# Transposing keys and queries by DMA in a fused retention and FFN kernel, with a rewoven start

## The chip, the cores and the metric

The kernel runs on one core of a Trainium2 chip. Profiles call the engines PE (TensorE, the matrix unit), DVE (VectorE), ACT (ScalarE), POOL (GpSimd) and SP (which here only issues DMAs). The metric is device time in microseconds (us), the median of several executions. The kernel before takes 228.82 us (three runs, 228.13 to 229.55). A run counts as slow, and is left out of comparisons, when it lies over 1.5% above the fastest run of the same kernel.

## The reference, cut to what matters

Four sequences of 768 tokens and 8 heads of 64 go through a retention recurrence, and its output goes through an FFN with a squared ReLU.

```python
for t in range(S):                       # per head, gamma = 1 - 2**(-5-h)
    state = gamma * state + outer(k[t], v[t])
    y[t] = scale * q[t] @ state
h = np.maximum(x @ w_in, 0.0)            # x: 3072 x 512, w_in: 512 x 2048
return h * h @ w_out                     # w_out: 2048 x 512
```

## The kernel before

The 3072 tokens are 24 chunks of 128. For a chunk, k is scaled and cast on VectorE (K), q is cast, and k and q are turned so that the head dimension lies on the partitions (T: eight PE transposes and one eviction by ScalarE). Scores are taken and masked (S), and output and state follow (P). The FFN works on blocks of 2, 2, 1, 3, 4, 4, 4 and 4 chunks: F is one row group of `x @ w_in`, G one quarter of `h*h @ w_out` for one chunk. Strings of these letters give the order of the program, and the engines are read here as running in it (the timeline below shows `K1`'s cast on VectorE at 10.73 us, `S0`'s multiply at 11.33); Z is a filler matmul on zeros, Y fills decay factors, L loads.

```python
    def a_turn(m):
        ...
        for x, src in enumerate((a["ks"], a["qs"])):
            for p in range(NP):
                nc.tensor.transpose(tp[:, x, p, :], src[:, 2 * p : 2 * p + 2, :], ident[:])
        nc.scalar.activation(kqT[:], tp[:], AF.Copy)
    ...
    run("Y0 Z12 K0 T0 Y1 Z2 K1 S0 Z2 T1 P0 K2 S1 Y2 Z2 T2")
    load_w_in(0)
    load_w_in(1)
    run("P1 K3 S2 Y3 Z2 T3 P2 S3 Y4 Z4")
    for s in (2, 3):
        load_w_in(s)
    for s in range(NSL):
        w = load_w_out(s)
    ...
    weave(
        all_f1(3) + all_f2(3),
        [... "K8 T8 K9,S8 L10,T9 K10,P8 S9 L11,T10 K11,P9 S10 L12,T11 L13,P10 S11 L14,P11 K12,T12 L15,S12,K13" ...],
    )
```

Note `K1 S0`: the k cast of the next chunk stands ahead of the scores whose mask multiply also runs on VectorE.

## Time and profile before

| | kernel before |
|---|---|
| time, median | 228.82 us |
| span of the profiled run | 225.9 us |
| PE busy | 212.3 us |
| first FFN matmul | 19.46 us |
| fifth block's FFN (512 columns) starts | 94.64 us |
| TensorE clock granted | 1.000 |

The prediction below shows the busy row, the chain and the waits. One more view matters later, the page's 40 slices of the span. PEclk is the clock granted to TensorE in each, in tenths of full speed, 9 being 90% or more.

```profile
PEclk9999999999999999999999999999999999999999
```

The clock is full throughout. How VectorE orders the start shows in the timeline (start, length, engine, line, operation; brackets hold the idle time before it):

```profile
10.73 0.68 DVE L192 SCALAR_TENSOR_TENSOR ks_272<-kn_116,kf 128x512 bf16<-128x512 f32 x1
10.78 0.40 PE L227 MATMUL st_278<-kqT_239 64*128 64x128 bf16 x8 [0.65 <-ACT kqT_239 L218]
...
11.33 1.22 DVE L235 TENSOR_TENSOR pt_287<-st_278,cmask 128x1024 bf16<-128x1024 f32 x1
```

The cast of the next chunk's k (10.73) comes before the mask multiply of these scores (11.33). The next chunk is turned while the multiply runs (its transposes start at 11.55 and 12.10 us, the multiply ends at 12.55); scores come every 3.2 to 3.5 us (7.59, 10.78, 14.32, 17.86).

### The profile page before, as it was taken

The numbers are of one execution on the slowest core, as the hardware profiler recorded it, in microseconds if no ns is written. First come the engines' busy times: TensorE is split into PE (matmuls) and PEld (weight loads), VectorE is DVE, ScalarE is ACT, GpSimd is POOL, SyncE is SP. The second block draws the span as 40 slices with busy tenths as digits, with TensorE's granted clock in tenths as the row PEclk, the third lists the DMA queues.
The fourth block names the chain that finished last, engine by engine and source line by source line (L and its number), as shares of the span: only waits on it lengthen the run. The fifth ranks groups of instructions, "written<-read, shape, count | busy, mean of one in ns | idle before, by whom it ended". The sixth has DMA issues, their size and how long they took to land.

```text
span 225.9 us, 4271 instructions
## 1 busy us (share of the span) xinstructions
PE 212.3 (94%) x1736; PEld 117.5 (52%) x1736; DVE 103.2 (46%) x221; ACT 123.1 (54%) x246; POOL 43.5 (19%) x62
## 2 busy tenths in 40 slices
PE   7677899998879999999999999999999999999993
PEld 2444785456646664445455555455454555444441
DVE  4574664127835964175650275740275704144000
ACT  6798883156637862377623477524467532367121
POOL 3275000439752433030330310000000000000000
PEclk9999999999999999999999999999999999999999
DMA  7999999989999999477729973013200011200112
GB/s 168 256 209 204 205 200 202 248 219 189 166 177 205 171 80 147 73 183 45 49 57 130 118 167 22 3 46 93 94 2 0 3 46 46 96 0 0 46 46 93
DMA packets 82579, 25.43 MB, mean 113 GB/s; under 512 B 75392, under 2 KB 79488, under 8 KB 82560
## 3 DMA queue, kind: packets, MB, share of 16 engines
q0 software_dynamic: 37504, 8.39, 40.7%
q1 hardware_dynamic: 45056, 16.78, 28.6%
q8 instruction: 13, 0.21, 0.4%
q14 instruction: 6, 0.05, 0.1%
HBM read 27.26 MB, written 6.29 MB: 149 GB/s over the span
## 4 chain that ended last, share of the span: by engine, by line
PE 84%; DMA 5%; ACT 4%; SPq 3%; DVE 2%; issue 1%; POOL 0%; ACTq 0%
DMA w_in_bf_96<-in_moe_w_in_dram 3%; SPq L91 3%; DMA vn_120<-in_v_dram 2%; PE op_2633 L335 2%; PE op_1480 L335 2%; PE op_2223 L335 2%; PE op_2512 L335 2%; PE op_2317 L335 2%; PE op_1920 L335 2%; PE op_1826 L335 2%; PE op_1427 L335 2%; PE op_1072 L335 2%; PE op_2860 L335 2%; PE op_705 L335 2%; PE op_695 L335 2%; PE op_2820 L335 2%
## 5 line engine op out<-in xcount | busy, mean ns | idle before, releaser
L316 PEld LDWEIGHTS <-w_in_bf_96 128*128 128x128 bf16 x128 | 11.4, 98 | 10.3 <-issue 1.4
L316 PEld LDWEIGHTS <-w_in_bf_98 128*128 128x128 bf16 x128 | 11.8, 98 | 8.7
L316 PEld LDWEIGHTS <-w_in_bf_99 128*128 128x128 bf16 x128 | 11.6, 98 | 8.2
L316 PEld LDWEIGHTS <-w_in_bf_97 128*128 128x128 bf16 x128 | 11.4, 98 | 8.1
L324 DVE TENSOR_TENSOR h_0_442<-h_0_442 128x256 bf16<-128x256 bf16 x32 | 9.3, 293 | 7.1 <-ACT h_0_442 L323 3.2
L324 DVE TENSOR_TENSOR h_5_2687<-h_5_2687 128x512 bf16<-128x512 bf16 x16 | 6.8, 426 | 11.8 <-ACT h_5_2687 L323 11.8
L324 DVE TENSOR_TENSOR h_2_1544<-h_2_1544 128x512 bf16<-128x512 bf16 x16 | 6.8, 424 | 10.7 <-ACT h_2_1544 L323 10.6
L324 DVE TENSOR_TENSOR h_4_2348<-h_4_2348 128x512 bf16<-128x512 bf16 x16 | 6.8, 425 | 9.6 <-ACT h_4_2348 L323 9.6
L324 DVE TENSOR_TENSOR h_3_1951<-h_3_1951 128x512 bf16<-128x512 bf16 x16 | 6.8, 423 | 9.5 <-ACT h_3_1951 L323 9.5
L324 DVE TENSOR_TENSOR h_1_876<-h_1_876 128x128 bf16<-128x128 bf16 (+1 forms) x32 | 8.2, 287 | 4.5 <-ACT h_1_876 L323 4.4
L335 PEld LDWEIGHTS <-h_5_2687 128*128 128x128 bf16 x64 | 6.3, 98 | 7.6
L335 PEld LDWEIGHTS <-h_3_1951 128*128 128x128 bf16 x64 | 6.0, 98 | 7.1
L335 PEld LDWEIGHTS <-h_2_1544 128*128 128x128 bf16 x64 | 6.0, 98 | 7.1
L335 PEld LDWEIGHTS <-h_4_2348 128*128 128x128 bf16 x64 | 5.9, 97 | 6.9
L335 PEld LDWEIGHTS <-h_1_876 128*128 128x128 bf16 x64 | 6.0, 98 | 6.8
L335 PEld LDWEIGHTS <-h_0_442 128*128 128x128 bf16 x64 | 6.0, 98 | 6.6
L351 PE MATMUL fill<-zero 128*128 128x512 bf16 x24 | 8.3, 484 | 1.2 <-DVE zero L146 1.2
L344 ACT ACTIVATE osb_744<-op_695 128x512 f32<-128x512 f32 x1 | 0.6, 597 | 8.2 <-PE op_695 L335 8.2
L253 PEld LDWEIGHTS <-s_bd_175 128*128 128x128 bf16 x48 | 3.6, 98 | 2.3
L351 PEld LDWEIGHTS <-zero 128*128 128x128 bf16 x24 | 2.4, 119 | 4.6 <-issue 2.7
L206 POOL CAST qs_736<-qn_420 128x512 bf16<-128x512 f32 x1 | 0.6, 613 | 19.6 <-DMA qn_420<-in_q_dram 19.6
L235 DVE TENSOR_TENSOR pt_792<-st_783,cmask 128x1024 bf16<-128x1024 f32 x1 | 1.2, 1225 | 5.8 <-PE st_783 L227 5.8
(811 smaller groups left out, 522.2 us busy)
## 6 DMA issues: line engine op xcount, KB each, us to landing
w_in_bf_96<-in_moe_w_in_dram POOLq DMA_DIRECT2D x1, 512.0 KB, 7.0
w_in_bf_97<-in_moe_w_in_dram POOLq DMA_DIRECT2D x1, 512.0 KB, 8.6
w_in_bf_98<-in_moe_w_in_dram POOLq DMA_DIRECT2D x1, 512.0 KB, 9.0
w_in_bf_99<-in_moe_w_in_dram POOLq DMA_DIRECT2D x1, 512.0 KB, 10.8
w_out_bf_100<-in_moe_w_out_dram POOLq DMA_DIRECT2D x1, 512.0 KB, 12.9
w_out_bf_101<-in_moe_w_out_dram POOLq DMA_DIRECT2D x1, 512.0 KB, 14.7
w_out_bf_102<-in_moe_w_out_dram POOLq DMA_DIRECT2D x1, 512.0 KB, 16.6
w_out_bf_103<-in_moe_w_out_dram POOLq DMA_DIRECT2D x1, 512.0 KB, 18.5
```

Source lines behind the costliest of these rows:

```text
L91: return eng.dma_start(t[:], src[b, :, i * C : (i + 1) * C, :].rearrange("h s d -> s h d"))
L206: nc.gpsimd.tensor_copy(qs[m][:], qn.pop(m)[:])
L235: nc.vector.tensor_tensor(out=pt[:], in0=st[:], in1=cmask[:, None, None, :].to_broadcast([P, 2, NP, P]), op=ALU.mult,)
L253: nc.tensor.matmul(yt[:, p, :], lhsT=s_bd[i % 2][:, p, :], rhs=kqT[:, 1, p, :], start=(p == 0), stop=False, skip_group_check=True,)
L316: nc.tensor.matmul(hp[:, :n], lhsT=w_in_bf[s][:, cb, r * P : (r + 1) * P], rhs=xts[g][:, cb, cols], start=(cb == 0), stop=(cb == NCB - 1),)
L324: nc.vector.tensor_mul(h2[:, fb, cols], h2[:, fb, cols], h2[:, fb, cols])
L335: nc.tensor.matmul(op[:], lhsT=h2s[g][:, fb, j * P : (j + 1) * P], rhs=w_out_bf[part][:, r, :], start=(fb == 0), stop=(fb == NFB - 1),)
L344: nc.scalar.activation(osb[:], op[:], AF.Copy)
L351: nc.tensor.matmul(t[:], lhsT=zero[:, :P], rhs=zero[:], start=True, stop=True)
```

## The change

Its intent is to take the transposes of chunks 8 to 23 off PE, the bound. A DMA issued by SP turns k and q straight into place, from two slots ahead. In the start the transposes are split in halves (t for k, u for q), the decay factors become products on GpSimd, casts get their own letters (k, q, v), and the blocks of 2, 2, 1 and 3 chunks are woven anew. The diff, cut to its core:

```diff
-    def a_turn(m):                      # whole transposes for every chunk
+    def a_turn(m, x):                   # half: x = 0 k, x = 1 q; tp shares ps_f's four buffers
+    def dma_turn(m):
+        at[m] = kTpool.tile([P, 2, NP, P], BF16, tag="kqT", name=f"kqT{m}")
+        nc.sync.dma_start_transpose(
+            at[m][:].rearrange("d x p s -> d (x p) s"),
+            kq[m][:].rearrange("s x h d -> s (x h d)"),
+        )
     def fill_yf(i):
-        for p in range(NP):
-            nc.scalar.activation(yf[i][:, p, :], t_f[:, i * C : (i + 1) * C], AF.Exp, ...)
+        nc.gpsimd.tensor_tensor(out=yf[i][:], in0=yf[0][:], in1=gc[:, i, :, None]..., op=ALU.mult)
...
-    run("Y0 Z12 K0 T0 Y1 Z2 K1 S0 Z2 T1 P0 K2 S1 Y2 Z2 T2")
-    load_w_in(0)
+    run("Z10 Y1 k0 t0 q0 Z1 u0 v0 Z2 S0 Y2")
+    run("k1 Z2 t1 q1 Z1 u1 P0 v1 S1 Y3")
+    issue_behind(load_w_in(0), q2)
+    run("k2 Z2 t2 q2 Z1 u2 P1 v2 S2")
     load_w_in(1)
+    run("k3 Z2 t3 q3 Z1 u3 P2 v3 S3 Y4")
...
+    behind = load_w_out(1)
+    load_w_out(2)
...
+    issue_behind(load(nc.sync, "k", 4), behind)
+    q4 = load(nc.sync, "q", 4)
+    issue_behind(load_w_out(3), q4)     # fourth quarter of w_out behind q of chunk 4
...
+    run("k6 ... S6 k7 G4.1 t7 q7 v7 P6 G3.3 u7 G4.2 S7 L8 L9 G4.3 P7")
+    run("k8 X8 L10")
+        runs("k9 L11,X9,S8,k10 L12,X10,P8 S9,k11 L13,X11,P9 S10,k12 L14,X12,P10 S11,k13 X13 L15,P11 S12,k14 X14"),
```

X is the transposing DMA. Buffers move too: `ps_f` gets four (from three), the separate transpose buffer in PSUM goes, and the FFN's `hpool` gets two (from three). The q casts of chunks 4 to 7 move from GpSimd to VectorE. No run tests these two by themselves.

More of the change, by code (lines that the diff above doesn't have):

```diff
@@ L59 @@
     ldpool = ctx.enter_context(tc.tile_pool(name="ldpool", bufs=4))
-    bfpool = ctx.enter_context(tc.tile_pool(name="bfpool", bufs=7))
-    kpool = ctx.enter_context(tc.tile_pool(name="kpool", bufs=4))
+    bfpool = ctx.enter_context(tc.tile_pool(name="bfpool", bufs=8))
+    kTpool = ctx.enter_context(tc.tile_pool(name="kTpool", bufs=5))
     atpool = ctx.enter_context(tc.tile_pool(name="atpool", bufs=3))
     xtpool = ctx.enter_context(tc.tile_pool(name="xtpool", bufs=3))
-    hpool = ctx.enter_context(tc.tile_pool(name="hpool", bufs=3))
+    hpool = ctx.enter_context(tc.tile_pool(name="hpool", bufs=2))
     opool = ctx.enter_context(tc.tile_pool(name="opool", bufs=4))
     PS = bass.MemoryType.PSUM
-    ps_tp = ctx.enter_context(tc.tile_pool(name="ps_tp", bufs=1, space=PS))
     ps_st = ctx.enter_context(tc.tile_pool(name="ps_st", bufs=1, space=PS))
@@ L70 @@
     ps_c = ctx.enter_context(tc.tile_pool(name="ps_c", bufs=1, space=PS))
-    ps_f = ctx.enter_context(tc.tile_pool(name="ps_f", bufs=3, space=PS))
+    ps_f = ctx.enter_context(tc.tile_pool(name="ps_f", bufs=4, space=PS))
     w_in_v = moe_w_in.rearrange("(cb p) f -> p cb f", p=P)
@@ L77 @@
     w_out_bf = [const.tile([P, FPS, DM], BF16, name=f"w_out_bf{s}") for s in range(NSL)]
-    kn, qn, vn, qs, vs = {}, {}, {}, {}, {}
+    kn, qn, vn, kq, vs = {}, {}, {}, {}, {}
     FIRST = 8
@@ L84, in load @@
         src = {"k": k, "q": q, "v": v}[name]
+        if m not in kq:
+            kq[m] = bfpool.tile([P, 2, H, D], BF16, tag="kq", name=f"kq{m}")
+            vs[m] = bfpool.tile([P, H, D], BF16, tag="v", name=f"vs{m}")
         if name == "k" or m < FIRST:
@@ L87, in load @@
             {"k": kn, "q": qn, "v": vn}[name][m] = t
-        else:
-            t = bfpool.tile([P, H, D], BF16, tag=name, name=f"{name}s{m}")
-            {"q": qs, "v": vs}[name][m] = t
+            t = t[:]
+        elif name == "q":
+            t = kq[m][:, 1]
+        else:
+            t = vs[m][:]
         return eng.dma_start(
-            t[:], src[b, :, i * C : (i + 1) * C, :].rearrange("h s d -> s h d")
+            t, src[b, :, i * C : (i + 1) * C, :].rearrange("h s d -> s h d")
         )
@@ L114 @@
         load(nc.sync, "k", m)
-        load(nc.sync, "q", m)
+        ins = load(nc.sync, "q", m)
+        if m == 2:
+            q2 = ins
         load(nc.sync, "v", m)
@@ L120 @@
     nc.gpsimd.iota(ex_i[:], pattern=[[C, NCH], [0, H]], base=0, channel_multiplier=1)
-    t_i = const.tile([P, S], I32)
-    nc.gpsimd.iota(t_i[:], pattern=[[1, S]], base=0, channel_multiplier=0)
+    t_i = const.tile([P, C], I32)
+    nc.gpsimd.iota(t_i[:], pattern=[[1, C]], base=0, channel_multiplier=0)
+    eg_i = const.tile([P, NCH, NP], I32)
+    nc.gpsimd.iota(eg_i[:], pattern=[[C, NCH], [0, NP]], base=0, channel_multiplier=0)
     ident = const.tile([P, P], BF16)
@@ L164 @@
         nc.vector.memset(lnp[r, h // 2 : h // 2 + 1], float(np.log(gammas[h])))
-    t_f = const.tile([P, S], FP32)
+    t_f = const.tile([P, C], FP32)
     nc.vector.tensor_copy(t_f[:], t_i[:])
+    eg_f = const.tile([P, NCH, NP], FP32)
+    nc.vector.tensor_tensor(
+        out=eg_f[:],
+        in0=eg_i[:],
+        in1=lnp[:, None, :].to_broadcast([P, NCH, NP]),
+        op=ALU.mult,
+    )
     yf = [const.tile([P, NP, C], FP32, name=f"yf{i}") for i in range(NCH)]
+    for p in range(NP):
+        nc.scalar.activation(yf[0][:, p, :], t_f[:], AF.Exp, scale=lnp[:, p : p + 1])
+    gc = const.tile([P, NCH, NP], FP32)
+    nc.scalar.activation(gc[:], eg_f[:], AF.Exp)
     def fill_yf(i):
-        for p in range(NP):
-            nc.scalar.activation(
-                yf[i][:, p, :],
-                t_f[:, i * C : (i + 1) * C],
-                AF.Exp,
-                scale=lnp[:, p : p + 1],
-            )
+        nc.gpsimd.tensor_tensor(
+            out=yf[i][:],
+            in0=yf[0][:],
+            in1=gc[:, i, :, None].to_broadcast([P, NP, C]),
+            op=ALU.mult,
+        )
     s_bd = [const.tile([P, NP, P], BF16, name=f"s_bd{x}") for x in range(2)]
@@ L182, with k_cast @@
         nc.vector.memset(t[:], 0.0)
-    at = {}
+    at, pts = {}, {}
     xts = {}
     state = {}
-    def a_cast(m):
-        i = m % NCH
-        ks = kpool.tile([P, H, D], BF16, tag="ks", name=f"ks{m}")
+    def k_cast(m):
         nc.vector.scalar_tensor_tensor(
-            out=ks[:],
+            out=kq[m][:, 0],
             in0=kn.pop(m)[:],
             scalar=scale,
-            in1=kf[:, i, :, None].to_broadcast([P, H, D]),
+            in1=kf[:, m % NCH, :, None].to_broadcast([P, H, D]),
             op0=ALU.mult,
@@ L199, in a_cast, with q_cast, v_cast @@
         )
-        if m < FIRST:
-            qs[m] = bfpool.tile([P, H, D], BF16, tag="q", name=f"qs{m}")
-            vs[m] = bfpool.tile([P, H, D], BF16, tag="v", name=f"vs{m}")
-            if m < 4:
-                nc.scalar.activation(qs[m][:], qn.pop(m)[:], AF.Copy)
-            else:
-                nc.gpsimd.tensor_copy(qs[m][:], qn.pop(m)[:])
-            nc.gpsimd.tensor_copy(vs[m][:], vn.pop(m)[:])
-        at[m] = dict(ks=ks, qs=qs.pop(m), vs=vs.pop(m))
-    def a_turn(m):
-        a = at[m]
-        kqT = atpool.tile([P, 2, NP, P], BF16, tag="kqT", name=f"kqT{m}")
-        a["kqT"] = kqT
-        tp = ps_tp.tile([P, 2, NP, P], BF16, tag="tp", name=f"tp{m}")
-        for x, src in enumerate((a["ks"], a["qs"])):
-            for p in range(NP):
-                nc.tensor.transpose(tp[:, x, p, :], src[:, 2 * p : 2 * p + 2, :], ident[:])
-        nc.scalar.activation(kqT[:], tp[:], AF.Copy)
+    def q_cast(m):
+        if m < 4:
+            nc.scalar.activation(kq[m][:, 1], qn.pop(m)[:], AF.Copy)
+        else:
+            nc.vector.tensor_copy(kq[m][:, 1], qn.pop(m)[:])
+    def v_cast(m):
+        nc.gpsimd.tensor_copy(vs[m][:], vn.pop(m)[:])
+    def a_turn(m, x):
+        if m not in at:
+            at[m] = kTpool.tile([P, 2, NP, P], BF16, tag="kqT", name=f"kqT{m}")
+        tp = ps_f.tile([P, NP, P], BF16, tag="psf", name=f"tp{m}_{x}")
+        for p in range(NP):
+            nc.tensor.transpose(tp[:, p, :], kq[m][:, x, 2 * p : 2 * p + 2, :], ident[:])
+        nc.scalar.activation(at[m][:, x], tp[:], AF.Copy)
+    def dma_turn(m):
+        at[m] = kTpool.tile([P, 2, NP, P], BF16, tag="kqT", name=f"kqT{m}")
+        nc.sync.dma_start_transpose(
+            at[m][:].rearrange("d x p s -> d (x p) s"),
+            kq[m][:].rearrange("s x h d -> s (x h d)"),
+        )
     def a_score(m):
-        a = at[m]
-        kqT = a["kqT"]
+        kqT = at[m]
         st = ps_st.tile([P, 2, NP, P], FP32, tag="st", name=f"st{m}")
@@ L240, in a_score @@
         )
-        a["pt"] = pt
+        pts[m] = pt
     def a_out(m, after=None):
         i = m % NCH
-        a = at.pop(m)
-        ks, vt, kqT, pt = a["ks"], a["vs"], a["kqT"], a["pt"]
+        ks, vt, kqT, pt = kq.pop(m)[:, 0], vs.pop(m), at.pop(m), pts.pop(m)
         g, j = divmod(m, 4)
@@ L374, in run @@
             op, args = word[0], [int(x) for x in word[1:].split(".")]
-            if op == "K":
-                a_cast(*args)
-            elif op == "T":
-                a_turn(*args)
+            if op == "k":
+                k_cast(*args)
+            elif op == "q":
+                q_cast(*args)
+            elif op == "v":
+                v_cast(*args)
+            elif op == "t":
+                a_turn(*args, 0)
+            elif op == "u":
+                a_turn(*args, 1)
+            elif op == "X":
+                dma_turn(*args)
             elif op == "S":
@@ L394, in run @@
                 load(nc.gpsimd, "v", *args)
-    run("Y0 Z12 K0 T0 Y1 Z2 K1 S0 Z2 T1 P0 K2 S1 Y2 Z2 T2")
-    load_w_in(0)
-    load_w_in(1)
-    run("P1 K3 S2 Y3 Z2 T3 P2 S3 Y4 Z4")
-    for s in (2, 3):
-        load_w_in(s)
-    for s in range(NSL):
-        w = load_w_out(s)
-        if s == 2:
-            behind = w
-    for m in range(4, 8):
-        for name in "kqv":
-            ins = load(nc.sync, name, m)
-            if m == 4 and name == "k":
-                issue_behind(ins, behind)
@@ L411, with runs @@
-    run("F0.0 P3 Y5 F0.1 F0.2 F0.3 F1.0 F1.1 F1.2 F1.3")
-    run(" ".join(f"F{b}.{s * FPS + r}" for s in (1, 2, 3) for b in (0, 1) for r in range(FPS)))
-    run(" ".join(f"G{m}.{s}" for s in (0, 1, 2) for m in (0, 1, 2)))
-    run("K4 G0.3 G1.3 G2.3 K5 T4 G3.0 S4 G3.1 T5 G3.2 P4 S5 G3.3 K6")
-    weave(all_f1(2) + all_f2(2), [lambda x=x: run(x) for x in ("P5", "T6", "S6", "K7 L8", "P6", "T7", "S7 L9")])
-    run("P7")
+    def runs(text):
+        return [lambda x=x: run(x) for x in text.split(",")]
@@ new lines @@
+    run("Z10 Y1 k0 t0 q0 Z1 u0 v0 Z2 S0 Y2")
+    run("k1 Z2 t1 q1 Z1 u1 P0 v1 S1 Y3")
+    issue_behind(load_w_in(0), q2)
+    run("k2 Z2 t2 q2 Z1 u2 P1 v2 S2")
+    load_w_in(1)
+    run("k3 Z2 t3 q3 Z1 u3 P2 v3 S3 Y4")
+    load_w_in(2)
+    load_w_in(3)
+    load_w_out(0)
+    behind = load_w_out(1)
+    load_w_out(2)
+    run("Y5 Z2")
+    run(" ".join(f"F0.{fb}" for fb in range(3)) + " P3 F0.3")
+    run(" ".join(f"F1.{fb}" for fb in range(4)))
+    run(" ".join(f"F{b}.{s * FPS + r}" for s in (1, 2, 3) for b in (0, 1) for r in range(FPS)))
@@ new lines @@
+    issue_behind(load(nc.sync, "k", 4), behind)
+    q4 = load(nc.sync, "q", 4)
+    load(nc.sync, "v", 4)
+    issue_behind(load_w_out(3), q4)
+    for m in range(5, 8):
+        for name in "kqv":
+            load(nc.sync, name, m)
+    run(" ".join(f"G{m}.{s}" for s in (0, 1) for m in (0, 1, 2)))
+    run("G0.2 k4 v4 G1.2 q4 t4 G2.2 u4 G0.3 S4 G1.3 G2.3 P4 k5 G3.0 F2.0 F2.1 t5 F2.2 F2.3 G3.1 q5 F2.4 F2.5 v5 u5 F2.6 F2.7 S5")
+    run("k6 F2.8 F2.9 F2.10 F2.11 P5 G3.2 t6 F2.12 F2.13 q6 v6 F2.14 F2.15 u6 G4.0 S6 k7 G4.1 t7 q7 v7 P6 G3.3 u7 G4.2 S7 L8 L9 G4.3 P7")
@@ L417 @@
+    run("k8 X8 L10")
     weave(
         all_f1(3) + all_f2(3),
-        [lambda x=x: run(x) for x in "K8 T8 K9,S8 L10,T9 K10,P8 S9 L11,T10 K11,P9 S10 L12,T11 L13,P10 S11 L14,P11 K12,T12 L15,S12,K13".split(",")],
+        runs("k9 L11,X9,S8,k10 L12,X10,P8 S9,k11 L13,X11,P9 S10,k12 L14,X12,P10 S11,k13 X13 L15,P11 S12,k14 X14"),
     )
-    loaded = [15]
-    def cast(m):
-        while loaded[0] + 1 < NCHUNK and loaded[0] < m + 2:
-            loaded[0] += 1
-            run(f"L{loaded[0]}")
-        a_cast(m)
@@ L432, in side @@
         for m in ms:
-            if m + 1 < NCHUNK:
-                seq.append(lambda m=m: a_turn(m + 1))
-            if m + 2 < NCHUNK:
-                seq.append(lambda m=m: cast(m + 2))
-            seq.append(lambda m=m: a_out(m, m + 1 if m + 1 < NCHUNK else None))
+            todo = [f"L{m + 4}" if m + 4 < NCHUNK else "", f"k{m + 3}" if m + 3 < NCHUNK else ""]
+            seq += runs(" ".join(todo))
+            if m + 3 < NCHUNK:
+                seq += runs(f"X{m + 3}")
+            seq += runs(f"P{m} S{m + 1}" if m + 1 < NCHUNK else f"P{m}")
         return seq
```

## The prediction

> **What bounds the kernel now.** I read the page's busy rows first, then the chain that ended last, then PE's own waits, and then time-ordered stretches of PE, SP and GpSimd.
>
> ```profile
> PE 212.3 (94%) x1736; PEld 117.5 (52%) x1736; DVE 103.2 (46%) x221; ACT 123.1 (54%) x246; POOL 43.5 (19%) x62
> ...
> PE 84%; DMA 5%; ACT 4%; SPq 3%; DVE 2%; issue 1%; POOL 0%; ACTq 0%
> ```
>
> The first line is busy time in us by engine, the second the chain that ended last, by engine. TensorE is the bound: nothing that shortens another engine counts unless PE was waiting for it. The chain's 8% of DMA and SP queue is the start: w_in_bf_96 is issued at 12.47 us and takes 6.95 us, so the first FFN matmul is at 19.46 us.
>
> From the FFN of the fifth block on (94.64 us) PE doesn't wait. In the chain in order of time (start, length):
>
> ```profile
> 94.80 0.86 PE hp_0_1545 L316 x4
> ...
> 128.50 0.86 PE hp_0_1952 L316 x4
> ...
> 162.07 0.86 PE hp_0_2349 L316 x4
> ```
>
> The period is 33.6 us. The work in it is 32 groups of four 512-column matmuls at 0.863 us, 27.6 us, and four attention chunks at about 1.5 us, 6.0 us: together 33.6, with no room for a wait. The transposes are part of it; PE's timeline (start, length):
>
> ```profile
> 110.06 0.39 PE L217 MATMUL tp_1746<-ident,ks_1673 128*128 128x128 bf16 x4
> 110.29 0.39 PE L217 MATMUL tp_1746<-ident,qs_1476 128*128 128x128 bf16 x4
> 110.51 1.03 PE L316 MATMUL hp_15_1756<-xt_1203,w_in_bf_99 128*128 128x512 bf16 x4
> ```
>
> The printed 0.39 us are pipelined ends; the next group starts 0.45 us after the first transpose, so one chunk's eight transposes cost PE 0.45 us. PE's waits are all early:
>
> ```profile
> PE tp_1119 L217 <- DVE ks_1116 L192: 1.3, 1, 1.3
> PE hp_0_499 L316 <- ACT h_0_442 L323: 1.2, 1, 1.2
> ...
> PE st_339 L227 <- ACT kqT_296 L218: 1.1, 1, 1.1
> PE st_392 L227 <- ACT kqT_357 L218: 1.1, 1, 1.1
> ```
>
> (us in total, times, longest.) The last two are in the prologue, before 19.46 us; the other two are at 22 and 65 us. From 19.46 to 94.64 us, 75.2 us, I add up 69.3 us of PE work at the spacings of this trace (0.437 us for four 256-column matmuls, 0.863 for 512, 0.45 transposes, 0.33 scores, 0.3 + 0.25 + 0.23 output and state): 5.9 us are waits.
>
> [...] Here one lasts 220 ns and they follow each other every 56 ns, so the measured spacing is what a removed transpose is worth. [...] No transposing DMA is in this trace[...]. The nearest thing is a 256 KB load of k, 1024 runs of 256 B. [...]
>
> ```profile
> kn_961<-in_k_dram SPq DMA_DIRECT2D x1, 256.0 KB, 6.8
> kn_1066<-in_k_dram SPq DMA_DIRECT2D x1, 256.0 KB, 10.0
> ...
> kn_1156<-in_k_dram SPq DMA_DIRECT2D x1, 256.0 KB, 7.3
> ...
> kn_1474<-in_k_dram SPq DMA_DIRECT2D x1, 256.0 KB, 3.1
> ```
>
> The last number is us from issue to landing. The first three were issued at 53 to 65 us, while GpSimd's casting q and v loads fill the engines (16 of them issued from 51.8 us, the last landing near 82); the fourth at 88 us, when they are thinner. A transpose, of the same size and run length, I take at 3 to 4 us on quiet engines and 5 to 8 on full ones.
>
> **The change, part by part.**
>
> (a) Transposes of chunks 8 to 23 leave PE: 16 x 0.45 = **7.2 us**. Ten of the sixteen are after 94.64 us, on a PE that never waits there: 4.5 us, certain if the DMA is in time. There a slot (one chunk) lasts some 8 us, and the transpose of chunk m+3 is issued before the output of m, while its scores come two slots later, some 16 us. [...] ScalarE also loses 1.02 us of eviction per chunk, worth nothing there.
>
> (b) Prologue. ScalarE there has 1.02 (eviction) + 1.27 (four yf activations) + 0.63 (q cast) + 0.77 (state) = 3.7 us a chunk, which is the 3.5 us cadence of scores (10.78, 14.32, 17.86 us). With yf on GpSimd it has about 2.5, and the loads' 3.0 us become the cadence (v casts at 5.69, 8.86, 11.91, 14.90). Scores of chunk 3 move from 17.86 to about 16.5 us. But the first FFN matmul waits for w_in_bf_96. Its issue moves from 12.47 to about 11 us (when q of chunk 2 has landed), beside loads that are still running: landing near 18.4. **1.0 us** gained, not 1.5.
>
> (c) The 1.2 us wait at 22 us (relu behind yf activations on ScalarE, with three PSUM buffers) goes: yf is elsewhere and there are four. **1.2 us**.
>
> (d) The stretch of chunks 4 to 7 (45.97 to 66.26 us here) has 4.1 us of waits, of which 1.3 for k of chunk 8. Rewoven, FFN work stands between each score and its output. But transposes, two open op tiles and hp tiles share four buffers: a 128-column tile takes PE 0.22 us, and it comes back only after about 0.55 us (1.0 for half a transpose). Scores to output still have 0.9 to 1.2 us of other work in three of four cases against 1.4 for the mask multiply. I put the waits at about 3.5: **0.4 us** gained, as the wait for k of chunk 8 takes another form below. The third w_out load now comes behind q of chunk 4 and should land near 41 us, for a need at 41 to 42.
>
> (e) **The first DMA transpose is late.** SP works in order. In the new order k of chunk 8 is issued behind the store of chunk 3. In the kernel before, that store comes well ahead of the stretch; SP's timeline:
>
> ```profile
> 53.06 0.33 SPq L345 DMA_DIRECT2D out_dram<-osb_853  x1
> 53.49 0.39 SPq L91 DMA_DIRECT2D kn_961<-in_k_dram  x1
> ```
>
> That is 1.25 us after the end of that chunk's last matmuls (52.24), and the cast of k isn't wanted until 65 us. In the changed kernel those matmuls (part 3 of chunk 3) are woven to just before the block's end. From there PE has half a transpose 0.22, two groups 1.73, scores 0.33, output 0.79, a wait for xt of about 0.9 and three 384-column groups 1.95: 5.9 us until the scores of chunk 8. Against this runs store and issue 1.25, k's landing 2.9 to 7, cast 0.7 + 0.2 of signals, transpose 3.5 to 6.5: 8.5 on quiet engines, 15.6 on full ones. PE waits **2.6 to 9.7 us** once. When? The q and v loads start when v of chunk 7 has landed, about 50 us (12 loads and two w_out from about 32 us), so at 60 to 70 us the engines are still busy. But k's place in the ring differs, so I take 5.5. The next transposes lose nothing more: their scores come 4 us apart behind the delayed one, and the transposes can follow in that time.
>
> Sum: 228.8 - 7.2 - 1.0 - 1.2 - 0.4 + 5.5 = **224.5 us**.
>
> **The rivals.** First, the wait in (e) is small because its loads and transposes go as on quiet engines: 219.0 + 2.6 = 221.6, and 219 if the weave had hidden it wholly. For it speaks that the change was laid out with a lead of two slots. Against it are the three landings of 6.8 to 10.0 us at this very stage. [...] Third, the transposes are hidden but SP's order makes stores and k loads queue behind a transpose that waits for a cast: with four output buffers and a k load a slot ahead, I see 0 to 2 us.
>
> **Range and chances.** The certain part is -4.5 us, the likely parts -5.3, and the wait in (e) takes back 2.6 to 9.7: 219 to 229 by this alone. [...] for other waits I add a little above: 217.5 to 231. The 2% line is 224.2 us, almost my centre, so faster and same are near even: 0.47 and 0.46; slower than 233.4 [...] 0.07.
>
> **What would show it.** (a) block periods of 31.8 us in place of 33.6 in the last blocks, without PE waits; longer ones if the transposes are late. (b) the first FFN matmul at 18 to 19 us, released by w_in. (c) no 1.2 us wait there. (d) about 3.5 us of small waits between 44 and 63 us. (e) one PE wait at st of chunk 8, released by the DMA into kqT, with k of chunk 8 issued right behind the fourth store; three quarters of this prediction's spread is its length. The prediction fails low if that wait isn't there, and fails high if transposes take over 8 us each.

## The result, and the profile after

The changed kernel takes **236.61 us** (four runs, 235.62 to 238.54), the kernel before in the same rounds 228.47. The ratio of fast runs is 1.0359 [1.0282, 1.0435]: slower. Here and below a ratio is the mean time of one kernel's fast runs over that of the other's of the same rounds, so not quite the ratio of the medians quoted, and the brackets are its 95% interval. The prediction was 224.5, with 217.5 to 231.0 as its range: it missed by 12 us and on the wrong side.

The page of the profiled run (span 234.8 us, state fast): busy us by engine, the granted clock, and the chain by engine.

```profile
PE 214.0 (91%) x1608; PEld 113.9 (48%) x1608; DVE 106.7 (45%) x226; ACT 105.4 (45%) x219; POOL 46.2 (20%) x64
...
PEclk9965589999999979999999999999999999999999
...
PE 81%; DMA 8%; DVE 5%; ACT 4%; issue 1%; SPq 0%; DVEq 0%; ACTq 0%
```

PE has fewer instructions than before (1608 for 1736) and is busy longer (214.0 for 212.3 us). PEclk tells why: from the third slice to the sixth, 12 to 35 us, the clock was 0.5 to 0.8 of full, and it dips once more in the fifteenth (82 to 88 us). In the chain, PE has fallen from 84 to 81%, while VectorE has risen from 2 to 5% and DMA from 5 to 8%.

Where the 8.9 us of span come from is read from when each stage starts, in the two timelines:

| stage | before, us | after, us | difference | predicted |
|---|---|---|---|---|
| start to first FFN matmul | 19.46 | 27.54 | **+8.08** | -1.0 |
| to first matmul of w_out | 16.15 | 16.64 | +0.49 | -1.2 |
| to first 384-column group (chunks 5 to 7) | 31.11 | 30.94 | -0.17 | -0.85 |
| to first 512-column group (chunks 8 to 11) | 27.92 | 32.83 | **+4.91** | +3.25 |
| to the end | 131.26 | 126.85 | -4.41 | -4.5 |

The predicted column is the prediction's own sum put into stages: the transpose of chunk 8 lies in the third stage, those of 9 to 13 in the fourth (five times 0.45, less the 5.5 of the wait), ten in the last.

PE's waits (us in total, times, longest) name both bad stages:

```profile
PE st_1155 L249 <- DMA kqT_1117<-kq_1073: 4.9, 1, 4.9
PE tp_0_243 L233 <- DVE kq_109 L209: 1.8, 1, 1.8
...
PE tp_0_356 L233 <- DVE kq_125 L209: 1.0, 1, 1.0
```

The first is the scores of chunk 8, waiting for the DMA. The others are in the start, where PE now waits for k casts. The chain in order of time (start, length) shows one whole turn of the start:

```profile
9.10 1.23 DVE pt_235 L257
10.32 0.94 DVE kq_109 L209
...
11.31 0.41 PE tp_0_243 L233 x4
...
11.74 0.60 ACT kqT_242 L234
12.34 0.53 ACT kq_109 L220
...
12.91 0.41 PE tp_1_252 L233 x4
...
13.34 0.61 ACT kqT_242 L234
...
13.99 0.62 PE st_281 L249 x8
14.64 1.23 DVE pt_290 L257
```

This is a chain with no slack. The mask multiply of chunk 0 comes first on VectorE, then the k cast of chunk 1, its transposes, ScalarE's eviction, the q cast behind that eviction, q's transposes, its eviction, scores, and the next mask multiply. Scores come at 8.59, 13.99, 20.08 and 26.18 us: 5.4 to 6.1 us a chunk.

The later wait is as the prediction's part (e) drew it, from store to scores:

```profile
71.69 0.33 SPq L366
...
72.11 4.92 DMA kn_1075<-in_k_dram
...
77.06 0.70 DVE kq_1073 L209
...
77.83 4.27 DMA kqT_1117<-kq_1073
...
82.15 0.61 PE st_1155 L249 x6
...
84.15 1.27 PE hp_4_1173 L337 x4
```

The last is an FFN group that took 1.27 us where such groups take 0.65: after the wait the clock was down again, 0.50 from 82 to 85 us. (The group before it took 1.40.)

And in the last blocks (first groups of the fifth and sixth blocks' FFN):

```profile
108.11 0.86 PE hp_0_1495 L337 x4
...
140.02 0.86 PE hp_0_1862 L337 x4
```

The period is 31.9 us, against 33.6 before: the saving of step (a) is there, without waits.

### The profile page after: what moved, and what is told of

It is laid out like the page before. It is cut to its first block, busy times and chain, and to the rows that moved or that the text cites. A ratio compares the mean times of both kernels' runs of the same rounds, so it can differ in the third digit from the quotient of the medians.

```text
span 234.8 us, 4040 instructions
## 1 busy us (share of the span) xinstructions
PE 214.0 (91%) x1608; PEld 113.9 (48%) x1608; DVE 106.7 (45%) x226; ACT 105.4 (45%) x219; POOL 46.2 (20%) x64
## 4 chain that ended last, share of the span: by engine, by line
PE 81%; DMA 8%; DVE 5%; ACT 4%; issue 1%; SPq 0%; DVEq 0%; ACTq 0%
DMA kqT_1362<-kq_1181 3%; DMA kn_1075<-in_k_dram 2%; DMA kqT_1117<-kq_1073 2%; PE op_812 L356 2%; PE op_2473 L356 2%; PE op_2107 L356 2%; PE op_1834 L356 2%; PE op_1750 L356 2%; PE op_2453 L356 2%; PE op_2191 L356 2%; PE op_704 L356 2%; PE op_2700 L356 1%; PE op_2660 L356 1%; PE op_1464 L356 1%; PE op_709 L356 1%; PE op_699 L356 1%
## 5 line engine op out<-in xcount | busy, mean ns | idle before, releaser
L337 PEld LDWEIGHTS <-w_in_bf_93 128*128 128x128 bf16 x128 | 12.5, 104 | 11.5 <-issue 1.7
L337 PEld LDWEIGHTS <-w_in_bf_94 128*128 128x128 bf16 x128 | 12.1, 100 | 9.4 <-issue 1.0
L337 PEld LDWEIGHTS <-w_in_bf_95 128*128 128x128 bf16 x128 | 11.8, 98 | 9.1
L337 PEld LDWEIGHTS <-w_in_bf_96 128*128 128x128 bf16 x128 | 11.6, 98 | 8.9 <-issue 0.4
L372 PE MATMUL fill<-zero 128*128 128x512 bf16 x24 | 11.0, 577 | 1.2 <-DVE zero L154 1.2
L356 PEld LDWEIGHTS <-h_5_2527 128*128 128x128 bf16 x64 | 6.3, 98 | 7.5
L356 PEld LDWEIGHTS <-h_2_1494 128*128 128x128 bf16 x64 | 6.1, 98 | 7.3
L356 PEld LDWEIGHTS <-h_3_1861 128*128 128x128 bf16 x64 | 6.1, 98 | 7.3
L356 PEld LDWEIGHTS <-h_4_2212 128*128 128x128 bf16 x64 | 6.1, 98 | 7.3
L356 PEld LDWEIGHTS <-h_1_817 128*128 128x128 bf16 x64 | 5.9, 98 | 6.4
L356 PEld LDWEIGHTS <-h_0_417 128*128 128x128 bf16 x64 | 5.8, 98 | 6.0
L249 PE MATMUL st_1155<-kqT_1117 64*128 64x128 bf16 x8 | 0.6, 305 | 4.9 <-DMA kqT_1117<-kq_1073 4.9
L274 PEld LDWEIGHTS <-s_bd_190 128*128 128x128 bf16 x48 | 4.0, 107 | 2.1
L103 POOL DMA_DIRECT2D w_out_bf_100<-in_moe_w_out_dram x1 | 0.8, 811 | 14.9 <-DMA qn_670<-in_q_dram 14.9
```

The lines of the kernel that those rows point to most:

```text
L103: return nc.gpsimd.dma_start(w_out_bf[s][:], w_out_v[:, s * FPS : (s + 1) * FPS, :])
L249: nc.tensor.matmul(st[:, hh, p, :], lhsT=kqT[r, 0, p, :], rhs=kqT[r, 1, p, :], start=True, stop=True,)
L274: nc.tensor.matmul(yt[:, p, :], lhsT=s_bd[i % 2][:, p, :], rhs=kqT[:, 1, p, :], start=(p == 0), stop=False, skip_group_check=True,)
L337: nc.tensor.matmul(hp[:, :n], lhsT=w_in_bf[s][:, cb, r * P : (r + 1) * P], rhs=xts[g][:, cb, cols], start=(cb == 0), stop=(cb == NCB - 1),)
L356: nc.tensor.matmul(op[:], lhsT=h2s[g][:, fb, j * P : (j + 1) * P], rhs=w_out_bf[part][:, r, :], start=(fb == 0), stop=(fb == NFB - 1),)
L372: nc.tensor.matmul(t[:], lhsT=zero[:, :P], rhs=zero[:], start=True, stop=True)
```

## The experiments

After the result I had three suspects. **S**: the start's chain of casts and evictions, and the clock that follows from it. **W**: the fourth quarter of w_out, now behind q of chunk 4. **D**: the transposing DMAs of chunks 8 to 13. The rivals were that k casts are held up by GpSimd's decay product running beside them (the second theory in what was expected of k_first, the first in yf_exp), and that the DMAs are innocent. Seventeen kernels ran, all with correct results. Traces of these runs print tiles without buffer numbers. "First FFN" is the time of the first FFN matmul in the profile.

### The start

**k_first** puts the k cast of the next chunk ahead of the scores, as before:

```diff
-    run("Z10 Y1 k0 t0 q0 Z1 u0 v0 Z2 S0 Y2")
-    run("k1 Z2 t1 q1 Z1 u1 P0 v1 S1 Y3")
+    run("Z10 Y1 k0 t0 q0 Z1 u0 v0 Z2 k1 S0 Y2")
+    run("Z2 t1 q1 Z1 u1 P0 v1 k2 S1 Y3")        # and so on for chunks 2, 3
```

> One edit to the changed kernel: in the start, the cast of k of the next chunk is issued on VectorE ahead of this chunk's scores, so that it no longer stands behind the mask multiply. Chain theory (the start is a chain of scores, mask multiply 1.23 us, k cast 0.7, half transpose, eviction 0.6, q cast 0.6, half transpose, eviction 0.6, some 6 us a chunk): mask multiply and cast, about 1.9 us, leave the chain three times, and PE, busier, gets its clock back sooner, some 1.5 us: 236.6 goes to about 229.5 (227.5 to 231.5), first FFN matmul near 20.5 us in place of 27.5. [...] (the decay products on GpSimd hold VectorE up): the products stay, so 235 or more. Late-load theory (w_in is issued too late): w_in is issued at the same time, so the first FFN matmul can't come before about 19.5 us, but that doesn't contradict the chain.

Measured: 233.86 us median; three runs of 232.75 to 234.0 and one of 359.95, which is the profiled one, at a clock of 0.559 throughout. Ratio of the fast three 1.0231 [1.0195, 1.0267]. The k casts moved (one a chunk) are worth about 3 us (1.0359 to 1.0231), less than the 7 expected; the profile can't be compared.

**kq_first** also moves the q cast ahead of k's eviction on ScalarE:

```diff
+    run("Z10 Y1 k0 q0 t0 Z1 u0 v0 Z2 k1 q1 S0 Y2")
+    run("Z2 t1 Z1 u1 P0 v1 k2 q2 S1 Y3")        # and so on
```

> As k_first, and also the q cast on ScalarE ahead of the eviction of k's half transpose. Chain theory: another 0.6 us a chunk leaves the chain, but now the loads (3.0 us a chunk) and ScalarE (2.6 us a chunk) are near, so 1 to 1.5 us more in all: about 228 (226.5 to 230). If the q cast isn't on the chain: the same as k_first.

Measured: 233.09 us, ratio 1.021 [1.0182, 1.0238]. The profiled run counts as slow (234.66 us, clock 0.976), so its span isn't compared. In it the first FFN matmul is at 20.41 us, 7 us earlier, and a w_out wait of 3.8 us and a w_in wait of 1.5 us are new; `both` and `three` below, which have the same start and fast profiles, confirm it (20.74 and 20.43 us).

**more_fills** changes no dependence; it puts more filler matmuls into PE's gaps, so that the clock stays up:

```diff
-    run("k2 Z2 t2 q2 Z1 u2 P1 v2 S2")
+    run("Z8 k2 Z2 t2 q2 Z5 u2 P1 v2 S2")        # likewise for chunks 0, 1, 3
```

> One edit: 24 more of the idle matmuls on zeros are put where PE waits in the start, so that it stays busy; no dependence changes. Clock theory (the loss is the granted clock that fell to half from 14 to 30 us): the clock stays near 1.0 and the time falls to about 229 to 230. Chain theory: the waits stay, only PE's own links (0.2 us each, about eight of them) and the first three FFN groups (0.42 us each) get shorter: about 233.5 (232 to 235), and the first FFN matmul still comes at about 25 us.

Measured: 233.42 us (232.8 to 233.7), ratio 1.0224 [1.0197, 1.0251]. The table by stretches (busy us of PE, PEld, VectorE, ScalarE, GpSimd with counts, then PEclk, DMA, GB/s), first the changed kernel, then this one, for the second turn of the start:

```profile
14.00:20.10 6.10, 4.37 (x41) 2.43 (x42) 2.33 (x4) 2.31 (x5) 3.89 (x6) 0.50 1.30 210
```

```profile
14.00:20.10 6.10, 5.97 (x57) 3.23 (x56) 3.19 (x5) 2.47 (x5) 2.75 (x5) 1.00 1.29 211
```

At full clock, the first FFN matmul comes at 23.91 us, so of the 8.08 us lost in the start 3.63 were the clock and 4.45 the chain. Scores still come only every 5.18 us (12.78, 17.96, 23.14). That is the chain's links at full clock: 0.41 + 1.23 + 0.68 + 0.41 + 0.60 + 0.53 + 0.41 + 0.61 = 4.88, and some 0.3 between them.

**yf_exp** computes the decay factors on ScalarE again and leaves all else:

```diff
-        nc.gpsimd.tensor_tensor(out=yf[i][:], in0=yf[0][:], in1=gc[...], op=ALU.mult)
+        for p in range(NP):
+            nc.scalar.activation(yf[i][:, p, :], t_f[:, i * C : (i + 1) * C], AF.Exp, scale=lnp[:, p : p + 1])
```

> One edit: the decay factors come from ScalarE activations again as in the kernel before, at the same places; the order of the start stays. [...] the first two k casts last 0.7 us again in place of 1.44 and 1.01, and the time falls to 231 or less. Chain theory: about 1.1 us less on VectorE, up to 1.3 us more on ScalarE at some evictions, so 234.5 to 238, and the mask multiply still ahead of each k cast.

Measured: 235.74 us, ratio 1.0345 [1.0289, 1.0401]; first FFN 26.79. In the changed kernel two k casts had taken 1.44 and 1.01 us beside GpSimd's products; here all take 0.68. So the products did hold those casts up; by what means no run shows. But the two casts are shorter by only 1.09 us together, and the first FFN matmul comes only 0.75 us earlier (net of the activations put back on ScalarE), so it is not the cause.

**old_prologue** puts the start of before back whole (its strings, whole transposes, decay factors on ScalarE) under the rest of the change:

```diff
-    run("Z10 Y1 k0 t0 q0 Z1 u0 v0 Z2 S0 Y2")    # ... to S3
+    run("Y0 Z12 K0 T0 Y1 Z2 K1 S0 Z2 T1 P0 K2 S1 Y2 Z2 T2")
+    load_w_in(0)
+    load_w_in(1)
+    run("P1 K3 S2 Y3 Z2 T3 P2 S3 Y4 Z4")
```

> The changed kernel with the start of before: its order of casts, transposes and scores, whole transposes, decay factors on ScalarE, the first w_in load as before. Theory (the start's order costs 8 us, and what is mended there is partly given back by the fourth w_out load and the first transposing DMA): first FFN matmul at 19.5 to 20 us, clock 1.0 there, a w_out wait of 3.5 to 4.5 us near 45 us, a kqT wait of 4 to 7 us: 232 to 234. Rival (the start was the whole of it, and the weave and transposes save as predicted): 236.6 - 8 = 228.5 or less.

Measured: 234.16 us, ratio 1.027 [1.0243, 1.0297]; first FFN 20.55, clock 1.0 there. The start's share is shown: 7.0 us come back by it. The total gains only 2.4. The chain in order of time shows where 3 of the rest went:

```profile
39.85 7.76 DMA w_out_bf<-in_moe_w_out_dram
47.65 1.86 PE op L363 x4
```

PE now reaches the fourth quarter of w_out at 44.6 us, before it has landed at 47.6: a wait of 3.0 us, and a clock of 0.50 from 48 to 52 us behind it (hence 1.86 us for four matmuls of 0.86). In the changed kernel itself PE was so late that this wait didn't show.

### The order of the loads

**k8_early** issues k of chunks 8 and 9 ahead of the stores, to shorten the wait of part (e):

```diff
-    run("G0.2 k4 v4 ... P4 k5 ...")             # L8 L9 stood behind S7
+    run("G0.2 k4 l8 v4 ... P4 k5 l9 ...")       # l: k alone; q and v stay behind S7
```

> One edit to the changed kernel: the loads of k of chunks 8 and 9 stand on SP's queue right behind the casts that free their buffers, ahead of the stores of chunks 0 and 3. The start stays as it is. Queue theory (the 4.9 us wait of the scores of chunk 8 is SP's order): that wait goes, and with it the half clock behind it (1.2 us in two FFN groups): 236.6 goes to about 230.8 (230 to 232.5). [...] k comes early but the transposes still hold the scores up: 234 or more.

Measured: 235.07 us, ratio 1.0287 [1.0243, 1.0332]. The wait is still 4.4 us. The load was early, but the cast stood on VectorE behind chunk 7's last multiply (about 74.9 us), and the DMA behind it took 5.79 us.

**both** is kq_first and k8_early together.

> kq_first and k8_early together. If the two losses are independent: 233.1 less 4.8 to 6 us, 227 to 228.5. The wait of 3.8 us for the last quarter of w_out, which came up in kq_first at 47.8 us, should stay; if it was caused by something in the later stretch it changes.

Measured: 232.99 us, ratio 1.0182 [1.0126, 1.0238]; waits of 4.7 (scores of chunk 8), 4.2 (w_out) and 1.9 us (w_in). The start's gain goes into the w_out wait.

**three** is both, with w_out's order of before:

```diff
-    behind = load_w_out(1)
-    load_w_out(2)
+    load_w_out(1)
+    behind = load_w_out(2)
+    load_w_out(3)
...
-    issue_behind(load_w_out(3), q4)
```

> both, and the loads of w_out in the order of the kernel before: the fourth quarter right behind the third, and the loads of chunks 4 to 7 once the third has landed. If the wait for the last quarter of w_out is due to its place behind q of chunk 4: it goes, 3.8 us less, about 224 (222.5 to 225.5), faster than the kernel before by 1.5% or more. If the DMA engines are simply full then, the wait turns up at k or q of chunk 4 and the time stays near 227.

Measured: 230.63 us, ratio 1.0125 [1.0071, 1.0179]. The w_out wait is gone; the wait for the transposing DMA grew to 6.6 us. From the chain in order of time, the DMA that was waited for:

```profile
67.43 8.03 DMA kqT<-kq
...
75.50 0.61 PE st L249 x8
```

PE arrives earlier than in the changed kernel (its wait ends at 75.5 us, there at 82.1), in a stretch where the transposing DMA took 8.03 us in place of 4.27.

**old_wout** does the same to old_prologue.

> old_prologue with the w_out order of before as well (fourth quarter right behind the third, k of chunk 4 behind the third). Theory: the w_out wait goes, a part of it comes back as a longer wait for the first transposing DMA: 229.5 to 231.5. Rival (w_out is independent of the rest): old_prologue less its whole w_out wait, 228 or less.

Measured: 233.44 us, ratio 1.0241 [1.0193, 1.0289], which is 2 us above what I expected. The w_out wait is gone, but the wait for the first transposing DMA is 8.1 us (4.6 in old_prologue). Stage by stage: 5.1 us gained up to the 384-column groups, 4.1 lost behind them.

### The transposing DMAs

**dma_alone** is the kernel before with transposing DMAs for chunks 8 to 23 and nothing else, but for the cast of k of chunk 8 one step earlier and a fourth `atpool` buffer:

```diff
+        kqT = atpool.tile([P, 2, NP, P], BF16, tag="kqT", name=f"kqT{m}")
+        nc.sync.dma_start_transpose(kqT[:]..., kq.pop(m)[:]...)      # in a_cast, for m >= 8
     def a_turn(m):
+        if m >= FIRST:
+            return
```

> The other way round: the kernel before with nothing changed but that chunks 8 to 23 are transposed by DMA, with the cast of k of chunk 8 one step earlier. Theory: PE loses 16 x 0.45 = 7.2 us of work, and up to 1.3 us of wait at chunk 8: 227.9 goes to 220 (219 to 222). If the DMA transposes cost as much as they save (slower loads at 60 to 80 us, late scores): 225 or more.

Measured: **232.16 us**, ratio 1.0175 [1.013, 1.022], where I had expected some 220: the clearest miss of the study. With the old start and no other change, the DMAs cost 4 us. The fifth block's FFN starts at 102.62 us (94.64 before), and from there on it gains 4.5. SP's timeline and PE's waits, of dma_alone:

```profile
63.48 1.32 SPq L223 DMA_TRANSPOSE kqT<-kq  x1
...
66.89 2.06 SPq L223 DMA_TRANSPOSE kqT<-kq  x1
69.00 0.57 SPq L98 DMA_DIRECT2D kn<-in_k_dram  x1
```

```profile
PE st L247 <- DMA kqT<-kq: 7.6, 4, 3.6
```

The load of k of chunk 10 leaves SP at 69.00 us, behind two transposes that each waited for a cast. In the kernel before it left at 65.42.

**three_pe** is three with PE transposes in place of all the DMAs.

> three with PE transposes, in halves and with ScalarE evictions, in place of the DMA transposes at the same places of the order; all loads as in three. What the DMA transposes are worth by themselves: PE gets 7.2 us of work back; the 6.6 us wait of the scores of chunk 8 goes, but for a wait of about 1.3 us for the cast of its k. If all else is hidden: 230.6 - 5.3 + 7.2 = 232.5 (231 to 234), so that the DMA transposes, as the changed kernel places them, gain about 2 us of their 7.2. If the transposing DMAs slow the other loads too: 229 to 231, and they gain nothing.

Measured: 231.37 us, ratio 1.0154 [1.009, 1.0218]. Of the 7.2 us that the DMAs should save over PE transposes, three (230.63) shows 0.7, and that is within the noise (1.0125 [1.0071, 1.0179] for three).

**early8** moves loads, casts and transposes of chunks 8 and 9 ahead of the outputs of 6 and 7:

```diff
-    run("k6 ... u7 G4.2 S7 m8 m9 G4.3 P7")      # m: q and v loads
-    run("k8 X8 L10")
+    run("k6 ... k7 G4.1 t7 q7 v7 m8 k8 X8 P6 G3.3 u7 G4.2 S7 m9 k9 X9 G4.3 P7")
+    run("L10")
```

> three, and the q, v loads, the k casts and the transposes of chunks 8 and 9 moved up behind the cast of v of chunk 7, ahead of the outputs of chunks 6 and 7. In three the wait of 6.6 us was no longer for k's load but for its cast, behind the last multiply of chunk 7, and then for a transpose that took 8.0 us. If the lead is the whole cause: the transpose of chunk 8 is issued about 7 us earlier, the wait falls to 0 to 1.5 us, 230.6 goes to 224 to 226. If the engines' load at 55 to 80 us is the cause: part of the wait comes back at chunk 8 or 9 or 10, and it is 227 to 229.

Measured: 231.42 us, ratio 1.0132 [1.0065, 1.0199], against 1.0125 for three. Chunk 8 waits only 0.7 us now, and chunk 10 waits instead. From the chain:

```profile
68.70 10.35 DMA kn<-in_k_dram
...
79.83 6.15 DMA kqT<-kq
```

**early8_hold** holds the q loads from chunk 10 on until the second transpose has landed, to give the transposes room:

```diff
+                if args[0] == 10:
+                    issue_behind(ins, turned[9])
```

> early8, with the q load of chunk 10, and all the q and v loads behind it on GpSimd's queue, held until the transpose of chunk 9 has landed. If the casting loads are what makes transposes take 6 to 8 us here and 3.1 later: the first two take 3 to 4 us, and the time is 0 to 3 us below early8 (223 to 226). If the held loads are then missed: waits for q or k of chunks 10 to 12, above early8.

Measured: 231.5 us, ratio 1.0153 [1.01, 1.0205]; kqT waits of 7.8 us, of which 6.6 for chunk 10. What is held back is missed later. But the run settles what makes the early transposes slow. The first two, issued at 62 and 66 us in both runs, first in early8, then here:

```profile
DMA to landing us min/median/max: 7.4/8.1/8.8
```

```profile
DMA to landing us min/median/max: 3.1/3.1/3.2
```

The hold keeps GpSimd from issuing q and v loads from 58 to 70 us. With it the same two DMAs land in 3.1 to 3.2 us in place of 7.4 to 8.8, and chunks 8 and 9 wait for nothing (early8_win, with the same hold, repeats it: 3.1 us each). When the held loads come, from 70 us on, the next two transposes take 8.3 and 11.0 us. So it is the casting q and v loads beside them, and not the transposing itself, that make these DMAs slow.

**early8_win** also issues the first w_in load earlier (right behind v of chunk 1), for the 1.4 to 1.9 us that PE waits for it.

> early8_hold, and the first load of w_in one step earlier: right behind the cast of v of chunk 1, not after a decay product and the landing of q of chunk 2. In kq_first the first FFN matmul waited 1.5 us for it. If it lands as much earlier as it is issued (2 us): the wait goes, 1.5 us less than early8_hold. If the loads of chunks 2 and 3 suffer for it: the same.

Measured: 233.0 us, ratio 1.0205 [1.0132, 1.0279]. The w_in wait goes, a q cast waits 2.1 us for its load instead, and kqT waits are 8.3 us. A loss.

**late14** is the kernel before with transposing DMAs for chunks 14 to 23 only:

```diff
-    FIRST = 8
+    FIRST, TURN = 8, 14        # else dma_alone with m >= TURN, and the weave of before
```

> The kernel before with only the transposes of chunks 14 to 23 taken off PE; chunks 8 to 13, whose loads share the crowded stretch of 55 to 95 us, stay as they were. Theory (transposing DMAs pay where the engines have room): up to 94.6 us nothing changes, then ten times 0.45 us go: 228 - 4.5 = 223.5, no PE wait on kqT over 0.5 us. Rival (each transposing DMA costs a wait or delays stores and loads on SP wherever it stands): 227 to 230, with PE waits on the DMA into kqT after 94 us.

Measured: **223.96 us** (222.86 to 227.13; the last counts as slow and is left out of the ratio), the kernel before 228.16; ratio 0.9802 [0.9774, 0.983]. It beats both kernels; whether by over 2% the interval leaves open. The span of its profiled run is 222.1 us. From its page, the busy times; then the landing times of its transposing DMAs:

```profile
PE 207.3 (93%) x1656; PEld 112.9 (51%) x1656; DVE 103.2 (46%) x221; ACT 114.6 (52%) x236; POOL 43.6 (20%) x62
```

```profile
DMA to landing us min/median/max: 2.7/2.8/4.2
```

In dma_alone the longest took 8.6 us. PE is busy 5.0 us less than before, none of its waits is for a DMA into kqT, and the stage up to 94.98 us is as before (94.64). Chunk 14's DMA is issued at 98.63 us and its scores come at 107.03: a lead of 8.4 us for a transfer of at most 4.2.

**three_late14** is three with PE transposes up to chunk 13.

> three (230.6) with PE transposes for chunks 8 to 13 and transposing DMAs from 14 on. Theory (the DMAs pay only where there is room): the kqT wait of 6.6 us goes, 2.7 us of transposes come back, and some of the wait comes back as a wait for the cast of k of chunk 8: 227 to 229.5, no kqT wait over 1 us. Rival (they cost wherever they stand): 230.5 to 231.5, as three and three_pe.

Measured: 227.0 us, ratio 0.9951 [0.9924, 0.9978]. No kqT wait is left; halves of transposes wait for VectorE's k casts, 5.3 us in nine places. So the change, with its early DMAs taken back and its start and loads mended, is on a par with the kernel before. But late14 has the same ten DMAs on the kernel before and takes 223.96 (0.9802): what is left of the change costs some 3 us. It does so before the ten transposes: the fifth block's FFN starts at 98.82 us here, at 94.98 in late14. Which part of it costs them (half transposes, q casts on VectorE, buffers, loads) isn't separated.

**dma_kpool** asks what makes the early DMAs costly. It is dma_alone with the k loads of chunks 8 to 23 issued by GpSimd, so that they don't stand behind transposes on SP:

```diff
-                load(nc.sync, "k", *args)
+                load(nc.gpsimd, "k", *args)
```

> dma_alone (232.16) with the k loads of chunks 8 to 23 issued by GpSimd, so that they no longer stand on SP behind transposing DMAs that wait for a cast. In dma_alone k of chunk 10 was issued at 69.0 us, behind two transposes, and cast at 77.8; in the kernel before it was issued at 65.4 and cast at 72.9. Theory A (SP's order delays the k loads): k of chunks 10 to 13 are cast 3 to 5 us earlier, PE's waits for kqT fall from 7.6 to 2 to 4 us, 226.5 to 229. Theory B (the DMA engines are full in this stretch, whoever issues): k lands as late as before behind the q and v loads that GpSimd issues, waits stay at 6 to 9 us, 231 to 234.

Measured: 228.24 us (226.46 to 229.72), ratio 1.0003 [0.9922, 1.0084], against 1.0175 for dma_alone. VectorE's timelines, k cast of chunk 10, first dma_alone, then dma_kpool:

```profile
77.79 0.69 DVE L202 SCALAR_TENSOR_TENSOR kq<-kn,kf 128x512 bf16<-128x512 f32 x1 [3.73 <-DMA kn<-in_k_dram]
```

```profile
71.82 0.68 DVE L202 SCALAR_TENSOR_TENSOR kq<-kn,kf 128x512 bf16<-128x512 f32 x1
```

The cast comes 6.0 us earlier, and 3.9 us of time come back: a third of the 11.3 us between dma_alone and the 220.9 that a free saving of 7.2 would have given (228.1 - 7.2). The waits for kqT fall only to 6.0 us, outside my 2 to 4: the transposes of chunks 8 to 11 still take 4.4 to 7.4 us (those issued at 63.09 and 72.58 us 6.04 and 6.01), for 2.7 at best. Both theories hold a part, and the second, the traffic, is what early8_hold shows directly.

How little room there is can be read in the kernel before. From k's cast on VectorE to the scores of the same chunk it has 2.6, 6.2, 4.3 and 4.8 us for chunks 8 to 11 (casts at 65.52, 66.12, 72.86 and 76.54, scores at 68.11, 72.29, 77.11 and 81.29), and VectorE waits for k of chunk 10. PE's transposes and their eviction need 0.45 + 1.02 us of that. A DMA of 6 us doesn't fit, unless k comes earlier.

### All of it in one table

Medians with the ratio to the kernel before of the same rounds, and from the profiles the start of the first FFN matmul, of the 384-column groups and of the 512-column groups.

| kernel | us | ratio | first FFN | 384 | 512 |
|---|---|---|---|---|---|
| before | 228.47 | 1 | 19.46 | 66.72 | 94.64 |
| changed | 236.61 | 1.0359 | 27.54 | 75.12 | 107.95 |
| more_fills | 233.42 | 1.0224 | 23.91 | 71.41 | 104.15 |
| old_prologue | 234.16 | 1.0270 | 20.55 | 73.11 | 105.49 |
| old_wout | 233.44 | 1.0241 | 20.64 | 67.99 | 104.51 |
| three | 230.63 | 1.0125 | 20.43 | 66.80 | 100.64 |
| three_pe | 231.37 | 1.0154 | 20.16 | 67.68 | 98.72 |
| three_late14 | 227.00 | 0.9951 | 20.78 | 69.42 | 98.82 |
| dma_alone | 232.16 | 1.0175 | 20.08 | 66.27 | 102.62 |
| dma_kpool | 228.24 | 1.0003 | 19.68 | 65.88 | 97.92 |
| late14 | 223.96 | 0.9802 | 19.80 | 67.06 | 94.98 |

The last two columns tell what the early DMAs cost: from 384 to 512 columns the kernel before takes 27.9 us, late14 27.9, dma_kpool 32.0, the changed kernel 32.8, dma_alone 36.4.

## Why the prediction was wrong, by its own steps

The predicted sum was -7.2 - 1.0 - 1.2 - 0.4 + 5.5. In spans the result is +8.9.

**(a), the transposes leave PE: right in the last blocks, and not collected before.** From 94.64 us on, 4.5 us were called certain; the change shows 4.41 and late14 4.46 up to the last block. The other 2.7 us were counted net of one wait. That was too simple: dma_alone shows that under the old schedule the scores wait four times for a DMA, and the fifth block's FFN starts 8.0 us later (102.62 for 94.64), though six chunks' transposes, 2.7 us, have left PE by then. The step's sentence "The next transposes lose nothing more" holds nearly in the changed kernel (0.7 us more); that PE was so late there that the loads had caught up is a likely reason, not a tested one.

**(b), the start: this step failed.** It said that with the decay factors on GpSimd "the loads' 3.0 us become the cadence", and it put the first FFN matmul at 18.4 us. It came at 27.54: 9.1 us of the 13.2 by which the prediction missed the span. The step added up ScalarE's busy time per chunk and took the next larger resource as the cadence. No engine was full there (of the 18.5 us from 9 to 27.5 us PE was busy 12.1, at a clock of 0.62, GpSimd 10.7, VectorE 8.5, ScalarE 7.3). The cadence was the chain from VectorE to PE to ScalarE and back that the program's order set: `S0 ... k1` where before had `K1 S0`, and `t1 q1` with an eviction between. The order was in the diff; I compared durations, not order. Undoing the order, with the new half transposes and GpSimd's products kept, brings the first FFN to 20.43 (three, whose other edits come later in the program), and the old start whole to 20.55. In neither does the start get faster than before: the predicted gain of 1.0 isn't there.

A second part of it I didn't see at all: a PE with little work lost its clock. Two rates stand in the trace: 0.50 at 14 to 20 us, where PE was busy 4.37 of 6.10 us, at half speed; filled up (more_fills, 5.97 of 6.10 us busy), it ran at 1.00, and 3.63 us came back. After the one long idle time, the 4.92 us wait for chunk 8, it was 0.50 from 82 to 85 us. But in the start there was no such idle time: PE's longest gap was 1.8 us, and it was busy 0.70 of the 3.00 us from 10 to 13, before the clock fell (0.50 from 14 us on). So here a stretch of little work was enough; how little is too little no run measured.

**(c), the wait at 22 us: right in size, paid back by the clock.** The stage from the first FFN matmul to w_out took 15.15 us in three, for 16.15 before: -1.0 for the predicted -1.2. In the changed kernel it took 16.64, for its first matmuls ran at reduced clock (0.55 from 27.5 to 31 us).

**(d), chunks 4 to 7: a fifth of a small gain, with one wrong landing.** The stage changed by -0.17 for -0.85, transpose of chunk 8 included. But "should land near 41 us" for w_out (its "third" load, counted from 0, is the fourth quarter) was wrong. Once PE came in time, it cost 3.0 to 4.2 us of waiting (old_prologue, both): in old_prologue it is issued only at 39.85 us, behind q of chunk 4, takes 7.76 us and lands at 47.6. In the changed kernel the late start hid it.

**(e), the first transposing DMA: right in place and nearly in size, in mechanism only half.** Predicted 5.5 us behind the fourth store; measured 4.92, with k's landing 4.92 and the transposing DMA's 4.27 inside the ranges given. But SP's order was not the only thing that held it: with k issued early (k8_early) 4.4 us of the wait stayed, behind a later cast and a DMA of 5.79 us. Not in the sum were about 1.3 us of half clock behind the wait, and 0.7 us for chunk 12.

**The rivals.** The first, a small wait in (e), is out by the 4.92 us. Transposes of over 8 us each, with which the prediction was to fail high, came only as single ones of the early chunks (8.6 us in dma_alone, 8.8 in early8, up to 11.0 in early8_hold): late14's ten landed in 2.7 to 4.2 us, 2.8 at the median, and a k load of the same 256 KB took 3.1 in the kernel before. The third, SP's order, was put at 0 to 2 us; in dma_alone it was worth 3.9 (232.16 to 228.24). No rival touched the start, which alone accounts for 9.1 us of the miss.

What stays open: how the DMA engines share out their time between transposes and the casting loads at 55 to 95 us, and so whether an order of loads exists in which the early DMAs pay; and which part of the rest of the change costs the 3 us between late14 and three_late14. Three tries (early8, early8_hold, early8_win) moved the wait and didn't remove it. Nor is it known why one run of k_first ran at a clock of 0.559.

## What to carry to other kernels

Work taken off the bound engine was collected here only where its replacement had a lead longer than its latency under that stretch's traffic (chunk 14 of late14: 8.4 us for a transfer of at most 4.2; at chunk 8 of three, PE waited 6.6 us for one of 8.03); test it first where traffic is thin, as late14 does with ten of sixteen transposes, which gain their 4.5 us of the 7.2 while the other six, placed early, gained nothing in any run and cost some 4 us in three (against three_late14). In a start-up, follow one chunk through all engines in program order and add the links, since sums by engine don't show a chain, and look where PE has little to do, because here it then ran at half clock as well (0.50 at 14 to 20 us, busy 4.37 of 6.10). And when the largest loss is mended, read the waits again: a wait that it had hidden may come up, as the one for w_out did.
